# The head of a three-layer kernel on one core: which transfers are issued first and by which queue, the probabilities loaded once, and transposes of the identity placed by the planner

## The chip, the core and the metric

One core of one Trainium2 chip runs the whole program. The metric is device time in microseconds (us) of one execution; the table below gives the median of three timed runs. Engines are named as in the profile: PE (TensorE matmul), PEld (its weight loads), DVE (VectorE), ACT (ScalarE), POOL (GpSimd), SP (SyncE). A "q" behind a name (SPq) is the engine's instruction queue, from which transfers are issued.

## The reference, cut

```python
def _attn_ref(q, k, v, p):            # q, k, v: (4, 8, 576, 64), p: (4, 8, 32, 64)
    p_packed = sm_attn(p, k, v)       # softmax(p k^T / 8) v : 32 packed rows for each head
    return sm_attn(q, p_packed, p_packed)

def _moe_ref(x, domain_probs, w1, w2):        # x: (2304, 512), 4 experts, F = 1024
    p = domain_probs / (domain_probs.sum(-1, keepdims=True) + 1e-09)
    for e in range(E):
        out += p[:, e:e + 1] * (np.maximum(x @ w1[e], 0.0) @ w2[e])

def _moe2_ref(x, phi, w1, w2):                # 8 experts of 4 slots each
    logits = x @ phi                          # softmax over rows (dispatch), over slots (combine)
    slot_out[e] = np.maximum((d.T @ x)[e] @ w1[e], 0.0) @ w2[e]
    return c @ slot_out

def reference(**kwargs):                      # attention, then _moe_ref, then _moe2_ref
    return _moe2_ref(_moe_ref(_attn_ref(...)))
```

## The kernel before

The program is written out by hand in the order in which each engine shall work. The second attention is never formed in full: with packed rows `pkn` (32 for each head) and weights `a2` (softmax of q against them), the first layer's x @ w1 is a2 @ (pkn @ w1). `make_g(ci)` computes g = pkn @ w1 for one half expert (512 columns of w1, one transfer of 1 MB into a tile `w1` of which there is one buffer), splits it into two fp32r parts, and then issues the next w1 transfer. `mm1(s)` computes h = relu(a2 @ g) for 128 columns, times the probability of the expert (`pe_t`), which is `ht`; there are 32 such slots for each of the 4 batch entries. `logits(ci)` needs w2 @ phi in place of w2: `wphi_ops(n, ...)` makes it for one of 8 chunks of w2 (1 MB each, n = 0 to 7): four groups of four transposes on PE (`turn`, psum tile `w2t{n}_x`), each copied out by ACT (`put`), a projection by phi of 32 small matmuls (`project`, psum tile `pw`), one transpose back (`wp`), copied out twice by ACT. The chunks lie in 4 buffers `w2s`; chunk n + 4 is loaded when chunk n has been projected.

The head, which the change touches, is everything up to the first `mm1`: the attention of batch entry 0 for two groups g of four heads, `make_g(0)`, the normalised probabilities, and as many of the `wphi_ops` as fit. The attention of one group runs: k transposed in 32x32 blocks by DVE (`kf`), scores p k^T on PE (`sa`), maximum, exponential, normalisation (`mx`, `ex`, `norm`), transposes on PE (`turn`, psum `et`), p_packed on PE (`pv`), packed into `pkn`, q transposed by DVE (`qf`), scores q pkn^T on PE (`sb`), and a softmax over 32 rows by DVE, ACT and POOL (`nat`, `sub`, `xp`, `add`, `mul`, `fl`), whose result is split into `a2` (`hi` on ACT, `lo` on DVE). `place_ops` orders these steps: every step has an engine, an expected cost and its predecessors; the planner takes the step that could begin first and issues its instructions, so the order on each engine is fixed when the program is built, by the planner's numbers. Steps of rank 2 (the `wphi_ops`) fill in; what of them is not placed when the rest is done is left in `rest` and issued two at a time between the `mm1` slots (`wphi_rest`).

All transfers of the head are issued by SP in the order of the `load(...)` calls, but for the probabilities, which POOL issues: `load_probs` reads the same 36 KB four times, once for each 32 partitions. SP issues in order: a transfer that must wait holds all behind it. Behind the planned part SP issues p, k and v of batch entry 1 (`load_p(1)`, `load_two`, `load_v(1, 0)`), then the third w1 half (`w1_2`). Tiles in `hr` are the ring that later takes h; in the head its parts hold q, v, w2 and the attention's intermediate tiles, so many rows name `hr`.

## Time and profile before

| | us |
|---|---|
| median of 3 timed runs | 516.65 (515.19 to 517.91) |
| the profiled execution | 512.97 |
| its span (first to last instruction) | 511.2 |
| PE busy in the span | 467.6 (91%) |
| PE matmuls of the h products (L620) | 221.6 |
| DMA read | 98.78 MB |

The sums below are made against the profiled execution (512.97 us). The span is 1.8 us shorter than that execution; the median of the timed runs is 3.7 us longer. Times inside the trace count from the first instruction. A row of the time line gives start, duration, engine, line, operation, what it writes and reads, and in brackets how long its engine had waited and what ended the wait. A row of the chain of waits gives start, duration and what the end of the program was waiting for in that stretch.

### The profile page before, as it was taken

How to read it: one execution, taken by the hardware profiler on the slowest of the kernel's cores; microseconds unless marked ns; L12 is line 12 of the kernel's file. 1: busy time of each engine (PE TensorE's matmuls, PEld its weight loads, DVE VectorE, ACT ScalarE, POOL GpSimd, SP SyncE). 2: the span in 40 equal slices, each digit the busy share in tenths (PEclk: the TensorE clock that was granted, in tenths of full speed). 3: DMA queues.
4: the chain of work that ended last, by engine and by line, in shares of the span. 5: the costliest groups of instructions: out<-in, count | busy, mean ns of one | idle time of the engine just before them, and what ended most of it. 6: DMA issues, size and time to landing. Idle time of an engine off the chain costs nothing.

```text
span 511.2 us, 13177 instructions
## 1 busy us (share of the span) xinstructions
PE 467.6 (91%) x5572; PEld 332.1 (65%) x5572; DVE 295.0 (58%) x551; ACT 185.4 (36%) x446; POOL 204.4 (40%) x266
## 2 busy tenths in 40 slices
PE   6899899999999989999998999999999985999683
PEld 3778767778775767787665877865878755322142
DVE  4674346688762977778278788754866533140022
ACT  2476445434432433455133445432443200320023
POOL 3024333458743635595244449642765505000000
PEclk8799999999999999999998999999999996899986
DMA  8999634555430555732234522591934499699997
GB/s 200 388 315 288 255 131 140 139 133 166 139 112 3 164 159 147 184 132 86 82 130 130 131 83 83 179 345 58 357 136 165 163 346 418 267 403 394 385 382 251
DMA packets 61836, 104.36 MB, mean 204 GB/s; under 512 B 5904, under 2 KB 24848, under 8 KB 61776
## 3 DMA queue, kind: packets, MB, share of 16 engines
q1 hardware_dynamic: 61648, 103.36, 59.9%
q8 instruction: 44, 0.72, 0.6%
q0 software_dynamic: 128, 0.15, 0.2%
q14 instruction: 16, 0.13, 0.1%
HBM read 98.78 MB, written 4.72 MB: 202 GB/s over the span
## 4 chain that ended last, share of the span: by engine, by line
PE 69%; DMA 17%; DVE 6%; SPq 3%; ACT 2%; issue 1%; POOL 1%; ACTq 0%; POOLq 0%; DVEq 0%
PE h L620 36%; DMA w<-in_moe_w_dram 8%; PE pb L775 8%; PE lg L653 6%; PE g L585 6%; DMA hr<-in_moe_w_dram 4%; DMA ck<-in_moe_w_dram 3%; SPq L849 2%; PE w2t L260 2%; PE sa L358 2%; PE so L1246 1%; DMA hr<-in_v_dram 1%; PE tt L1133 1%; PE o L1284 1%; PE pw L275 1%; PE pv L455 1%
## 5 line engine op out<-in xcount | busy, mean ns | idle before, releaser
L631 POOL TENSOR_TENSOR ht<-ht,pe 128x288 f32<-128x288 f32 x192 | 153.0, 806 | 180.3 <-ACT ht L630 180.2
L620 PEld LDWEIGHTS h<-a,g 128*128 128x128 f32 x1536 | 206.6, 188 | 23.0 <-issue 14.6
L620 PE MATMUL h<-a,g 128*128 128x288 f32 x1536 | 221.6, 299 | 0.0
L630 ACT ACTIVATE ht<-h 128x288 f32<-128x288 f32 x192 | 79.0, 412 | 173.8 <-PE h L620 166.2
L641 DVE STREAM_TRANSPOSE hr<-ht 128x576 f32<-128x576 f32 x128 | 97.3, 763 | 45.2 <-POOL ht L631 41.8
L597 DVE TENSOR_TENSOR g<-g,g 128x512 fp32r<-128x512 f32 x64 | 40.9, 679 | 26.0 <-ACT g L595 26.0
L625 DVE SCALAR_TENSOR_TENSOR ht<-h,pe 128x288 f32<-128x288 f32 x64 | 28.0, 438 | 37.8 <-PE h L620 37.8
L595 ACT CAST g<-g 128x512 fp32r<-128x512 f32 x64 | 34.5, 589 | 28.5 <-PE g L585 28.5
L775 PE MATMUL pb<-hr,d 32*32 32x512 f32 x1152 | 40.6, 598 | 0.0
L585 PE MATMUL g<-w,pkn 64*32 64x512 f32 x512 | 35.8, 600 | 4.2 <-DMA w<-in_moe_w_dram 4.1
L653 PE MATMUL lg<-ht,wphi 128*32 128x288 f32 x512 | 38.3, 412 | 0.0
L653 PEld LDWEIGHTS lg<-ht,wphi 128*32 128x32 f32 x512 | 13.5, 109 | 33.2 <-POOL ht L631 22.5
L775 PEld LDWEIGHTS pb<-hr,d 32*32 32x32 f32 x1152 | 18.9, 103 | 14.3 <-issue 9.2
L1246 PE MATMUL so<-hr,hm 128*32 128x256 f32 (+1 forms) x136 | 18.5, 458 | 4.6 <-DMA hr<-in_moe_w_dram 4.6
L1267 DVE TENSOR_TENSOR rr<-sr,rr 32x256 fp32r<-32x256 f32 x4 | 1.7, 424 | 34.5 <-ACT rr L1265 34.5
L267 ACT COPY hr<-w2t 128x512 f32<-128x512 f32 x32 | 17.5, 598 | 5.3 <-PE w2t L260 5.2
L260 PE MATMUL w2t<-ident,hr 128*128 128x128 f32 x128 | 18.1, 288 | 0.2 <-ACT hr L267 0.2
L260 PEld LDWEIGHTS w2t<-ident,hr 128*128 128x128 f32 x128 | 15.4, 149 | 2.9 <-issue 0.9
L673 POOL COPY ps<-dpn 128x576 f32<-128x576 f32 x16 | 10.7, 667 | 13.5 <-DVE dpn L195 13.5
L789 DVE SCALAR_TENSOR_TENSOR tacc<-tacc,rsc,pb 128x512 f32<-128x512 f32 x12 | 8.2, 744 | 13.2 <-PE pb L775 13.2
L1246 PEld LDWEIGHTS so<-hr,hm 128*32 128x32 f32 x136 | 6.1, 116 | 13.5 <-DMA hr<-in_moe_w_dram 9.3
L1133 PE MATMUL tt<-fold,tacc 128*128 128x64 f32 x32 | 7.1, 423 | 7.7 <-POOL fold L1114 7.7
(161 smaller groups left out, 444.8 us busy)
## 6 DMA issues: line engine op xcount, KB each, us to landing
w<-in_moe_w_dram SPq DMA_DIRECT2D x32, 1024.0 KB, 5.1
hr<-in_moe_w_dram SPq DMA_DIRECT2D x40, 512.0 KB, 8.8
ck<-in_moe_w_dram SPq DMA_DIRECT2D x38, 512.0 KB, 7.6
hr<-in_moe_w_dram SPq DMA_DIRECT2D x8, 1024.0 KB, 9.9
k<-in_k_dram SPq DMA_DIRECT2D x16, 288.0 KB, 4.4
v<-in_v_dram SPq DMA_DIRECT2D x18, 192.0 KB, 6.3
q<-in_q_dram SPq DMA_DIRECT2D x12, 288.0 KB, 2.9
out_dram<-ob SPq DMA_DIRECT2D x8, 384.0 KB, 5.6
```

The source lines that it names most:

```text
L260: pe.transpose(st[x][:, 128 * dc : 128 * dc + 128], t[:, x, 128 * dc : 128 * dc + 128], ident,)
L585: pe.matmul(ps[g][c : c + 32, :], pkn_t[b][o : o + 64, g, hp, 0, :], t[o : o + 64, 2 * g + hp, :], start=True, stop=True, tile_position=(o ...
L595: act.copy(gg[:, 0, g], ps[g])
L597: dve.tensor_tensor(out=gg[:, 1, g], in0=ps[g], in1=gg[:, 0, g].bitcast(F32), op=ALU.subtract)
L620: pe.matmul(ps[:, :HS], gg[:, l, g, fs], m[:, ts], start=(g == 0 and i == 0), stop=(g == 1 and i == 2),)
L625: dve.scalar_tensor_tensor(out=ht[:, ts], in0=ps[:, :HS], scalar=0.0, in1=pr[:, ts], op0=ALU.max, op1=ALU.mult,)
L630: act.activation(out=ht[:, ts], in_=ps[:, :HS], func=AF.Relu)
L631: pool.tensor_tensor(out=ht[:, ts], in0=ht[:, ts], in1=pr[:, ts], op=ALU.mult)
L641: dve.transpose(out=hr[:, place(b, i), :, f0 : f0 + 32], in_=ht_t[s].rearrange("p (x t) -> p x t", t=32),)
L653: pe.matmul(lg_t[b][r][32 * x : 32 * x + 32, :HS], wphi[:, NFT * e + 4 * hf + x, :], ht_t[4 * ci + x][:, HS * r : HS * r + HS], start=(ch ...
L775: pe.matmul(pb[c][m : m + 32, :], d[o, x + par, :], hr[o, lo : hi + 1 : hi - lo, x + par, :], start=(x == 0), stop=(x == NBLK - 2), tile_p ...
L1246: pe.matmul(so[32 * e : 32 * e + 32, d0 : d0 + dw], hm[s][:, x + xl, e, :], cks[e][:, dw * xl : dw * xl + dw], start=(s == 0 and x + xl == 0),
```

## The change

Seven edits, all ahead of the first `mm1`:

1. p of batch entry 0 is issued by ACT as its first instructions, and no longer by SP.
2. SP begins with k. Then come phi and the first w2 chunk, then v and q of group 0 with the probabilities between them, v and q of group 1, w2 chunks 1 and 2, w1_0, w2 chunk 3. The planner counts 2.6 us for 1 MB and adds to each a time until it has landed (`late`).
3. k is transposed in two steps (`kf0`, `kf1`), each as soon as its half is there.
4. The probabilities are loaded once, into 32 partitions, by SP; they are normalised there in three DVE steps, and POOL copies them to the other 96 partitions (`copy_probs`).
5. During the head seven psum banks serve the planner instead of six.
6. The 16 identity transposes at the start (`warm`) go; instead, whenever the planner sees PE wait, it fills the wait with as many (`idle`), into bank 7. There are 17 at the start and 32 more in ten places.
7. Behind the head nothing else is written differently; the `wphi_ops` left over begin at another point.

```diff
-                sp.dma_start(
+                (sp if b else act).dma_start(
...
     def load_probs():
-        for c in range(4):
-            pool.dma_start(
-                dpn[32 * c : 32 * c + 32].rearrange("p b (r x) e -> p (b r) (x e)", r=2),
-                dprobs.rearrange("(b r t x) e -> t (b r) (x e)", b=NB, r=2, x=XR),
-            )
+        sp.dma_start(
+            dpn[0:32].rearrange("p b (r x) e -> p (b r) (x e)", r=2),
+            dprobs.rearrange("(b r t x) e -> t (b r) (x e)", b=NB, r=2, x=XR),
+        )
...
+    def copy_probs():
+        for c in range(1, 4):
+            pool.tensor_copy(dpn[32 * c : 32 * c + 32], dpn[0:32])
...
+            if o.eng == "PE":
+                idle(free.get("PE", 0.0), t)
+            free[o.eng] = t + o.cost
+            o.end = t + o.cost + o.late
...
+        @op(0, "DVE", 0.7, *landed("k0"))
+        def kf0():
+            flip("k", 0)
+
+        @op(0, "DVE", 0.7, kf0, *landed("k1"))
+        def kf1():
+            flip("k", 1)
             late("k")
...
+        load_p(0)
+        load(("p", 0), 0.0, lambda: None, late=3.6)
         for g in range(2):
...
+            for hp in range(2):
+                load((f"k{hp}", g), 0.3, lambda g=g, hp=hp: load_qk(k, "k", 0, g, hp), late=2.2)
...
-        wp = mm_ps("warm")
-        for _ in range(16):
-            pe.transpose(wp[:, :128], ident, ident)
+        def idle(t0, t1):
+            n = int((t1 - max(t0, 1.4)) / (0.213 if t1 < 6 else 0.109))
+            wp = bank(7, "warm") if n > 0 else None
+            for _ in range(n):
+                pe.transpose(wp[:, :128], ident, ident)
```

SP's queue from the last of the four k transfers on, before (`in_moe_w2_dram` is w2, `in_moe_w1_dram` is w1, `tacc` takes phi):

```order
L138 DMA k011_159<-in_k_dram 128x576
L147 DMA hr_109<-in_v_dram 32x8x192 x6
L138 DMA hr_109<-in_q_dram 128x576 x2
L244 DMA hr_109<-in_moe_w2_dram 128x4x512
L138 DMA hr_109<-in_q_dram 128x576 x2
L913 DMA tacc_107<-in_moe2_phi_dram 128x4x32
L244 DMA hr_109<-in_moe_w2_dram 128x4x512
L176 DMA w1_0_339<-in_moe_w1_dram 128x4x512
L244 DMA hr_109<-in_moe_w2_dram 128x4x512 x3
L176 DMA w1_1_490<-in_moe_w1_dram 128x4x512
L244 DMA hr_109<-in_moe_w2_dram 128x4x512
```

The same stretch now:

```order
L140 DMA k011_135<-in_k_dram 128x576
L924 DMA tacc_107<-in_moe2_phi_dram 128x4x32
L256 DMA hr_109<-in_moe_w2_dram 128x4x512
L149 DMA hr_109<-in_v_dram 32x8x192 x3
L184 DMA dpn_105<-in_moe_domain_probs_dram 32x8x36
L140 DMA hr_109<-in_q_dram 128x576 x2
L149 DMA hr_109<-in_v_dram 32x8x192 x3
L140 DMA hr_109<-in_q_dram 128x576 x2
L256 DMA hr_109<-in_moe_w2_dram 128x4x512 x2
L178 DMA w1_0_441<-in_moe_w1_dram 128x4x512
L256 DMA hr_109<-in_moe_w2_dram 128x4x512 x3
L178 DMA w1_1_585<-in_moe_w1_dram 128x4x512
```

p no longer stands in front of k; one w2 chunk stands ahead of v; w1_0 stands behind w2 chunks 1 and 2 instead of behind chunk 1; and w1_1 stands behind w2 chunk 5 instead of ahead of it.

PE in the attention of entry 0, from the transposes of the probabilities to the first `sb`, before (the last digit of `et`, `pv` and `sb` names is a half or group; `w2t0_x` are chunk 0's transposes):

```order
L419 MATMUL et000_229<-ident_103,hr_109 96x128 x4
L419 MATMUL et001_230<-ident_103,hr_109 96x128 x2
L455 MATMUL pv00_242<-hr_109 64x32 x24
L419 MATMUL et010_275<-ident_103,hr_109 96x128 x4
L419 MATMUL et011_276<-ident_103,hr_109 96x128 x2
L260 MATMUL w2t0_0_291<-ident_103,hr_109 128x128 x4
L260 MATMUL w2t0_1_297<-ident_103,hr_109 128x128 x4
L260 MATMUL w2t0_2_303<-ident_103,hr_109 128x128 x4
L455 MATMUL pv01_311<-hr_109 64x32 x24
L358 MATMUL sb000_342<-hr_109,pkn0_156 32x288
```

The same stretch now, from the last transposes of chunk 0 on:

```order
L272 MATMUL w2t0_3_246<-ident_103,hr_109 128x128 x4
L954 MATMUL warm_251<-ident_103 128x128 x4
L434 MATMUL et000_256<-ident_103,hr_109 96x128 x4
L434 MATMUL et001_257<-ident_103,hr_109 96x128 x2
L954 MATMUL warm_275<-ident_103 128x128 x5
L434 MATMUL et010_281<-ident_103,hr_109 96x128 x4
L434 MATMUL et011_282<-ident_103,hr_109 96x128 x2
L954 MATMUL warm_293<-ident_103 128x128
L470 MATMUL pv00_295<-hr_109 64x32 x24
L954 MATMUL warm_334<-ident_103 128x128 x9
L470 MATMUL pv01_344<-hr_109 64x32 x24
L370 MATMUL sb000_376<-hr_109,pkn0_142 32x288
```

Chunk 0's transposes moved from between the two `pv` to ahead of `et`, and identity transposes stand where they were and ahead of each step.

PE around the first h products, before (`h0_0` is slot 0, first half; `wp1` and `pw2` belong to w2 chunks 1 and 2):

```order
L260 MATMUL w2t2_3_513<-ident_103,hr_109 128x128 x4
L260 MATMUL w2t3_0_521<-ident_103,hr_109 128x128 x4
L291 MATMUL wp1_528<-ident_103,pt1_519 128x128
L260 MATMUL w2t3_1_530<-ident_103,hr_109 128x128 x4
L260 MATMUL w2t3_2_536<-ident_103,hr_109 128x128 x4
L275 MATMUL pw2_544<-hr_109,tacc_107 32x128 x16
L620 MATMUL h0_0_585<-a2_00_509,g0_388 128x288 x3
L620 MATMUL h0_0_585<-a2_01_541,g0_388 128x288 x3
L620 MATMUL h0_1_594<-a2_00_509,g0_388 128x288 x3
L620 MATMUL h0_1_594<-a2_01_541,g0_388 128x288 x3
L585 MATMUL g1_0_604<-w1_1_490,pkn0_156 32x512 x2
```

And now:

```order
L287 MATMUL pw1_528<-hr_109,tacc_107 32x128 x16
L954 MATMUL warm_550<-ident_103 128x128 x2
L272 MATMUL w2t3_0_553<-ident_103,hr_109 128x128 x4
L272 MATMUL w2t3_1_559<-ident_103,hr_109 128x128 x4
L303 MATMUL wp1_566<-ident_103,pt1_548 128x128
L272 MATMUL w2t3_2_571<-ident_103,hr_109 128x128 x4
L954 MATMUL warm_577<-ident_103 128x128
L272 MATMUL w2t3_3_579<-ident_103,hr_109 128x128 x4
L954 MATMUL warm_587<-ident_103 128x128 x3
L287 MATMUL pw2_591<-hr_109,tacc_107 32x128 x16
L272 MATMUL w2t4_0_611<-ident_103,hr_109 128x128 x4
L635 MATMUL h0_0_640<-a2_00_521,g0_505 128x288 x3
```

The fourth group of chunk 3 and the first of chunk 4 moved ahead of h0. Behind h0 follows in both programs the second g (`g1`, which needs w1_1), and now `pw3` stands between `g1` and slot 1. In the stretch up to the third g (`g2`) the new order has chunk 4's projection (`pw4`, `wp4`) too, which stands behind `g2` before.

## Rows read from the trace of the kernel before

**Rows 1.** Chain of waits, in order of time: start us, us, what.

```profile
14.43 11.93 DMA w<-in_moe_w_dram
...
44.70 7.88 DMA w<-in_moe_w_dram
52.72 1.09 PE g L585 x16
...
54.92 0.92 PE pw L275 x32
...
60.62 0.87 PE w2t L260 x8
61.49 1.59 PE h L620 x12
```

**Rows 2.** Busy time in stretches of the head and behind it; columns in the first line.

```profile
core 0: us, PE busy (x) PEld busy (x) DVE busy (x) ACT busy (x) POOL busy (x), PEclk, DMA share, GB/s
4.80:7.10 2.30, 0.01 (x1) 0.00 (x0) 0.78 (x1) 0.00 (x0) 0.76 (x3) 1.00 1.06 350
9.30:12.00 2.70, 2.55 (x40) 0.61 (x24) 1.90 (x5) 0.58 (x3) 0.00 (x0) 0.64 1.12 236
18.00:21.70 3.70, 3.70 (x20) 3.58 (x18) 2.44 (x5) 2.51 (x7) 0.67 (x1) 0.53 1.08 388
21.70:25.40 3.70, 3.66 (x114) 2.75 (x112) 2.55 (x8) 1.34 (x5) 0.00 (x0) 1.00 1.05 408
29.90:32.60 2.70, 2.49 (x25) 1.83 (x18) 2.60 (x5) 2.70 (x8) 0.00 (x0) 1.00 0.53 75
52.70:66.40 13.70, 12.80 (x166) 10.66 (x166) 5.22 (x8) 6.35 (x15) 3.41 (x5) 1.00 0.50 192
```

**Rows 3.** Time line of SP's queue, first 46 us.

```profile
0.74 1.81 SPq L159 DMA_DIRECT2D p<-in_p_dram  x4
2.60 1.87 SPq L138 DMA_DIRECT2D k<-in_k_dram  x4
...
16.33 14.21 SPq L244 DMA_DIRECT2D hr<-in_moe_w_dram  x3
30.64 0.45 SPq L176 DMA_DIRECT2D w<-in_moe_w_dram  x1
34.38 0.37 SPq L244 DMA_DIRECT2D hr<-in_moe_w_dram  x1
```

**Rows 4.** What SP's queue waited for, 0 to 53 us: us, times, longest.

```profile
SPq L244 <- PE pw L275: 12.5, 2, 9.3
```

**Rows 5.** DMA issues, KB, us to landing: to 53 us; at 30.6; at 34.4.

```profile
hr<-in_moe_w_dram SPq DMA_DIRECT2D x8, 1024.0 KB, 9.9
...
dpn<-in_moe_domain_probs_dram POOLq DMA_DIRECT2D x4, 36.0 KB, 3.3
...
w<-in_moe_w_dram SPq DMA_DIRECT2D x1, 1024.0 KB, 8.3
...
hr<-in_moe_w_dram SPq DMA_DIRECT2D x1, 1024.0 KB, 7.7
```

**Rows 6.** Time line of DVE and PE, single rows between 1 and 57 us.

```profile
1.36 3.45 PE L933 MATMUL warm<-ident 128*128 128x128 f32 x16 [1.36 <-POOL ident masks.py:199]
...
7.23 1.70 DVE L344 STREAM_TRANSPOSE hr<-k 128x576 f32<-128x576 f32 x2 [0.15 <-DMA k<-in_k_dram]
...
9.33 0.78 DVE L344 STREAM_TRANSPOSE hr<-k 128x576 f32<-128x576 f32 x1 [0.41 <-DMA k<-in_k_dram]
...
21.04 0.78 DVE L344 STREAM_TRANSPOSE hr<-hr 128x576 f32<-128x576 f32 x1 [1.19 <-DMA hr<-in_q_dram]
...
23.31 2.05 PE L358 MATMUL sb<-hr,pkn 32*32 32x288 f32 x64
...
36.81 0.76 DVE L542 TENSOR_TENSOR a<-hr,a 128x576 fp32r<-128x576 f32 x1 [0.80 <-ACT a L537]
...
37.38 1.86 PE L620 MATMUL h<-a,g 128*128 128x288 f32 x12
...
39.17 1.09 PE L585 MATMUL g<-w,pkn 64*32 64x512 f32 x16
...
52.72 1.09 PE L585 MATMUL g<-w,pkn 64*32 64x512 f32 x16 [1.56 <-DMA w<-in_moe_w_dram]
...
56.23 0.33 PE L291 MATMUL wp<-ident,pt 128*128 128x128 f32 x1 [0.44 <-ACT pt L286]
```

More of the change, by code (lines that the diff above doesn't have):

```diff
@@ L87, in mm_ps @@
     def mm_ps(name, keep=False):
-        i = min((i for i in range(6) if i not in kept), key=lambda i: idle_since[i])
+        i = min((i for i in range(nbank[0]) if i not in kept), key=lambda i: idle_since[i])
         clock[0] += 1
@@ L204, in __init__, with place_ops @@
             self.end = None
-    def place_ops(ops, lag=0.2):
-        free, banks_at, left = {}, [0.0] * 6, list(ops)
+    def place_ops(ops, idle, lag=0.2):
+        free, banks_at, left = {}, [0.0] * nbank[0], list(ops)
         while any(o.rank < 2 for o in left):
@@ L225, in place_ops @@
             t, _, n, o = first
-            o.end = free[o.eng] = t + o.cost
+            if o.eng == "PE":
+                idle(free.get("PE", 0.0), t)
+            free[o.eng] = t + o.cost
+            o.end = t + o.cost + o.late
             banks_at = sorted(banks_at)[o.take :] + [o.end] * o.give
@@ L366, in scores @@
             st["ps"] = ps
-        @op(0, "DVE", 1.5, *landed("k"))
-        def kf():
-            for hp in range(2):
-                flip("k", hp)
+        @op(0, "DVE", 0.7, *landed("k0"))
[4 more added lines that the diff above has]
+            flip("k", 1)
             late("k")
-        @op(2, "PE", 1.2, kf, take=2)
+        @op(2, "PE", 1.2, kf1, take=2)
         def sa():
@@ L891, in tile_packed_attention_moe_softmoe, with load @@
         ops = []
-        def load(key, mb, fn, rank=0, deps=()):
-            o = Op(0, "SP", 2.5 * mb, fn, deps, rank=rank)
+        def load(key, mb, fn, rank=0, deps=(), late=2.2):
+            o = Op(0, "SP", 2.6 * mb, fn, deps, rank=rank, late=late)
             ops.append(o)
@@ L961, in tile_packed_attention_moe_softmoe @@
         spread = spread_p(0)
-        ops.append(Op(0, "DVE", 1.7, norm_probs, [loads["k", 1]], rank=1))
+        probs = norm_probs()
+        ops.append(Op(0, "DVE", 0.48, lambda: next(probs), [loads["dp"]], rank=1))
+        ops.append(Op(0, "DVE", 0.87, lambda: next(probs), ops[-1:], rank=1))
+        ops.append(Op(0, "DVE", 0.38, lambda: next(probs, None), ops[-1:], rank=1))
+        ops.append(Op(0, "POOL", 1.2, copy_probs, ops[-1:], rank=1))
         ops.append(Op(0, "POOL", 0.7, lambda: next(spread), ops[-1:], rank=1))
@@ L976, in tile_packed_attention_moe_softmoe @@
                 after = Op(
-                    0, "SP", 2.5, lambda m=m: load_w2(m, w2s[m % W2_BUFS]), [], rank=2
+                    0, "SP", 2.6, lambda m=m: load_w2(m, w2s[m % W2_BUFS]), [], rank=2, late=2.2
                 )
@@ L981, in tile_packed_attention_moe_softmoe @@
             ops.append(Op(0, "NONE", 0.0, done, ops[-1:], rank=2))
-        rest = place_ops(ops)
+        rest = place_ops(ops, idle)
         for o in list(rest):
@@ L987, in tile_packed_attention_moe_softmoe @@
                 rest.remove(o)
+        nbank[0] = 6
         load_p(1)
```

38 lines of the change are left out of this document (21 added, 17 removed).

## The prediction

> **What bounds the kernel now.** I read the chain of waits first. In the head its long pieces are transfers: w1_0 is waited for from 14.43 on and lands 11.93 us later, at 26.36; w1_2 is issued at 44.70 and lands at 52.58, and the third g starts behind it at 52.72 [rows 1], after PE had stood idle for 1.56 us [rows 6]. Behind that point the chain is PE: from 52.7 to 66.4 PE works 12.80 of 13.70 us while the DMA engines are half idle [rows 2]. So the head is bound by when bytes arrive, the rest by PE, and an edit to the head is worth what it moves g2 (the third g, now at 52.72), plus any PE work that is done before g2 and formerly came behind it.
>
> Then I read the stretches for the state of the DMA engines. They are full early (share 1.06 to 1.12), at 236 GB/s while v moves and about 400 later (408 at 21.7 to 25.4), but from 29.9 to 32.6 they run at 0.53 and 75 GB/s [rows 2]: a hole. The queue of SP shows why. It sits on the row of 16.33 for 14.21 us, and behind it w1_1 is issued only at 30.64 [rows 3]; the wait is for `pw`, 9.3 us in one piece [rows 4], since w2 chunk 4 may be loaded only when chunk 0 has been projected, and chunk 0 came late. Besides, k is issued only at 2.60, behind p [rows 3]. These are two losses of DMA time that the change can touch: the start and the hole.
>
> **The change part by part**, as landing times, since these set the end.
>
> *Start.* k is issued at 0.74 in place of 2.60: 1.86 us earlier [rows 3]. Today the four k land up to 9.33, the last two 2.1 us behind the second (7.2) [rows 6], so 1.05 each; 0.30 MB (288 KB) at 408 GB/s [rows 2] would take 0.72. The four loads of the probabilities by POOL (36 KB each [rows 5]) run beside them and leave this stretch; p (0.13 MB) enters it from ACT's queue. Gain between 0 and 4 x 0.33 = 1.3; I take 1.0, because what leaves is as many bytes as what enters, but in smaller pieces. So the last k lands at 9.33 - 1.86 - 1.0 = 6.4 (bounds 6.1 to 7.5).
>
> The row says that the k transfers were slowed by others beside them. The Trainium skill, page "DMA: Bandwidth & Descriptors", section "Issuing engines are not separate DMA queues", has the rule against this edit: transfers started by different engines interleave on the same 16 DMA engines, and issuing from a second one saves only the issuing time. By that rule the last k would land at 7.4 and everything below 1.0 later; no row here has SP and ACT issuing together.
>
> *The same bytes in another order.* Between the last k (9.33) and the last q of group 1 (21.04) lie v, q, phi and one w2 chunk: 11.7 us [rows 6]. The new order moves the same set in this stretch, plus the single load of the probabilities, for which I put 0.4 (bounds 0.1, 36 KB at 408 GB/s, and 1.0). So the last q lands at 6.4 + 11.7 + 0.4 = 18.5. Then 1.05 MB pieces at 408 GB/s, 2.6 us each: w2_1 21.1, w2_2 23.7, w1_0 26.3, w2_3 28.9, w2_4 31.5, w2_5 34.1, w1_1 36.7. w1_0 is where it was (26.36), since a whole w2 chunk has been put ahead of it; that costs nothing, because w2 has to come anyway.
>
> *The hole.* w2_4 now needs `pw0`, which stands between the two `sb`, about 20 to 21: long before its turn at 28.9. w2_5 needs `pw1`, which stands behind g0: 26.3 + 1.09 + 1.0 = 28.5. Issued then, it has 3.0 us until its turn at 31.5. In the trace w1_1, issued into the hole at 30.64 just behind w2_4, landed 8.3 us later [rows 3, 5]; moving the two takes 5.2, so some 3.1 pass between an issue and its first bytes. That is even: I expect no hole worth counting, with nothing to spare. SP now holds w1_1 behind this wait.
>
> *The chain of the attention.* `sb` begins at 23.31, h0 at 37.38, a2 of group 1 is complete at 37.57 [rows 6]; from the last q (21.0) to that a2 are 16.5 us. PE is at the low clock in 18.0 to 21.7 (0.53, so near 1.2 GHz) and at 2.4 GHz from 21.7 on [rows 2]. After the last q at 18.5 the same chain ends at 35.0 at worst; the w2 transposes that stand between the `pv` today are ahead of them now, and `sb` starts some 2 us nearer to q, so about 33. h0 then starts near 33 instead of 37.38. That is ahead of w1_1, so this chain is hidden. The new wait is g1, directly behind h0: h0 ends near 35 and PE waits for w1_1 until 36.7. Of the 4 us that h0 gains, g1 (39.17 now [rows 6]) keeps 2.5.
>
> *From g1 to g2.* In the new order: g1 1.0, `wp2` 0.1, `pw3` 1.0, four h slots of 1.59, `wp3` 0.1, three groups of transposes at 0.87/2, `pw4` 1.0 and `wp4` with its wait 0.6 [rows 1, 6]: 1.0 + 0.1 + 1.0 + 6.4 + 0.1 + 1.3 + 1.0 + 0.6 = 11.5. So g2 at 36.7 + 11.5 = 48.2. It needs w1_2. Today that lands 10.5 us after w2_5 (34.38 + 7.7 = 42.1 [rows 5]; 52.58 [rows 1]), with p, k and v of entry 1 between; now the same set follows w1_1: 47.2. Hidden by 1.0.
>
> *Work moved ahead of g2.* `pw4` and `wp4` stand behind g2 now: 0.92, a wait of 0.44 and the transpose [rows 1, 6], 1.5 in all.
>
> *Cost at nothing.* Normalising 32 partitions takes DVE the same columns; POOL's three copies and the spread have until h0, some 15 us. The table load on ACT comes 1.8 us later, and ACT's first exponential needs the scores of k, which lands at 6.4 at the earliest for the last. The 33 more identity transposes: 3.45/16 = 0.22 us each at the start, 0.11 (0.87/8) at the full clock [rows 6, 1], 3.6 to 7.1 in all; they stand in waits for transfers, and up to g1 there are 1.7 us of slack. If that cover were missing, they would be the cost. The low clock of 9.3 to 21.7 (0.64, 0.53 [rows 2]) is paid in the shade of transfers already, so its going is worth only what the attention chain has above.
>
> **Sum.** 52.72 - 48.2 = 4.5, plus 1.5: 6.0; I take off 0.3 for the fillers and ACT's fuller queue around g1. The gain is 5.7: 512.97 becomes 507.3, and the median 516.65 becomes **511.0** (the median lies 3.7 above the profiled execution; I move both by the same amount).
>
> **The rivals.**
>
> *A, only the issue time is won at k*, or the probabilities cost 1.0 in the new place. Everything lands 1.0 later: gain 4.7, **512.0**. For it: p enters the stretch of k, in pieces as small as ever. Against: what leaves is of the same size.
>
> *B, the hole comes back* at w2_5, since SP must now wait for `pw1` before it can issue w1_1. For it: exactly this wait cost 9.3 us of SP's time [rows 4], and there is no margin. Against: `pw1` needs only w1_0 and copies of ACT that are early. A hole of 2.5, as now, gives 3.2: **513.4**.
>
> *C, the clock.* PE falls to the low clock after waits such as 4.8 to 7.1 (busy 0.01) and is there from 18.0 to 21.7 although it is busy [rows 2]. If identity transposes do not hold it up and PE works at 1.2 GHz from w1_0 on, then g0, `pw1`, four groups, `pw2`, one group and h0, 1.1 + 1.0 + 1.7 + 1.0 + 0.4 + 1.6 = 6.8, take 13.6; g1 starts at 39.9, 3.2 late: gain 2.5, **514.1**. Against: at 21.7 the clock was up again after work of the same kind.
>
> *D, slower: w1_0 is late.* Three 1 MB loads stand ahead of it instead of two, and w1_0 frees g0, that `pw1`, that w2_5, and that w1_1 behind it. From w1_0 at 27 on, each us costs one; from 33 the change is no gain. If all moved as slowly as v (236 GB/s [rows 2]), the 0.04 + 3.15 MB behind q would take 13.5 instead of 8.2, w1_0 would land at 32 and w1_1, with 5.2 for that chain (1.1 + 1.0 + 3.1) and two chunks of 4.4, at 46: g2 at 57.5, gain -3.3, **519.9**. Against: behind v the rate is 388 to 408 in two stretches [rows 2].
>
> **Chances.** The forecast 0.57 (its own range 509.5 to 512.5), A 0.16, B 0.13, C 0.08, D 0.03, and 0.03 for what I don't see. For 8 in 10 the range reaches from 508.3 (the last k at 6.1, a cheap load of the probabilities, no loss at g1, and the 1.4 us by which the timed runs differ) to 514.2 (B and C, partly). A measurement of this kernel tells some 0.5% (2.6 us) from no change: below 514.1 I put 0.82, above 519.2 0.04, and 0.14 between.
>
> **What would show it.** Right: k's last transposition near 6.5; no stretch of low DMA share before 45 us; the wait of SP for `pw` down from 9.3 to below 3; h0 near 33; PE waiting 1 to 3 us at g1 for w1_1, near 36.7; g2 near 48 without a wait. Behind g2 the two traces should run alike, 6 us apart. Wrong: w1_0 after 27.5, a hole between w2_4 and w2_5, a granted clock below 1 between 22 and 36, or time that is won at g2 and lost again later, for which I see no place in the trace.

## The result, and the profile after

The change makes the kernel slower by about half a per cent: 518.9 us in the median of 20 runs (511.9 to 523.9) against 514.5 for the kernel before (20 runs), with a ratio of 1.0055 and an interval of 1.0029 to 1.0082. Six of the 20 runs, of 520.3 us and more, the first profiled one among them (523.61), count as slow and are left out of the ratio; the median of the other 14 is 517.6. A later set of runs gave the same ratio, 518.0 against 514.5, 1.0055 (1.0019 to 1.0090). The forecast was 511.0, and faster.

The rows below are of a second profile of the changed kernel (518.08 us, span 516.3), whose head goes the same way as the first one's. The forecast times of the head beside what the two profiles show, in us from the first instruction:

| | before | forecast | after, 1st | after, 2nd |
|---|---|---|---|---|
| last k lands | 9.30 | 6.4 | 6.83 | 6.88 |
| last q lands | 21.01 | 18.5 | 22.76 | 21.72 |
| w1_0 lands | 26.36 | 26.3 | 30.82 | 29.87 |
| w2 chunk 5 issued | 34.38 | 28.5 | 35.80 | 34.78 |
| w1_1 lands | 38.98 | 36.7 | 45.38 | 44.18 |
| h0 begins | 37.38 | 33 | 40.06 | 39.01 |
| g1 begins | 39.17 | 36.7 | 45.51 | 44.32 |
| g2 begins | 52.72 | 48.2 | 59.08 | 57.79 |

I read the chain of waits first, as before [rows 1]. Chain of the changed kernel (start, duration, what):

```profile
2.15 4.91 DMA p<-in_p_dram
...
21.94 1.54 issue
23.49 0.71 PE pv L470 x7
...
35.24 8.94 DMA w<-in_moe_w_dram
44.18 0.14 issue
44.32 1.96 PE g L600 x16
...
57.86 1.02 PE g L600 x16
```

The long piece is w1_1, issued at 35.24 and 8.94 us under way; g1 hangs on it. w1_2, the long piece of before (7.88 us), no longer stands in the chain.

What SP's queue waited for up to 53 us, and its time line (start, duration; a row runs to the last issue of its group):

```profile
SPq L256 <- PE pw L287: 13.7, 3, 6.5
```

```profile
18.40 1.06 SPq L178 DMA_DIRECT2D w<-in_moe_w_dram  x1
19.51 15.64 SPq L256 DMA_DIRECT2D hr<-in_moe_w_dram  x3
35.24 0.46 SPq L178 DMA_DIRECT2D w<-in_moe_w_dram  x1
```

The wait for `pw` is there as before (12.5 us, 9.3 the longest [rows 4]), and as before w1_1 stands behind it. But w1_1 now stands behind chunk 5, which waits for `pw1`, where before it stood behind chunk 4, which waited for `pw0`. The row of 15.64 us ends with chunk 5's issue. The two issues between 34.5 and 35.7, with KB and the time to landing:

```profile
hr<-in_moe_w_dram SPq DMA_DIRECT2D x1, 1024.0 KB, 5.5
w<-in_moe_w_dram SPq DMA_DIRECT2D x1, 1024.0 KB, 8.9
```

Stretches of the head (columns in the first line); they answer to [rows 2]:

```profile
core 0: us, PE busy (x) PEld busy (x) DVE busy (x) ACT busy (x) POOL busy (x), PEclk, DMA share, GB/s
9.00:12.00 3.00, 3.00 (x49) 1.05 (x39) 1.64 (x4) 0.30 (x1) 0.00 (x0) 1.00 1.11 282
12.00:16.00 4.00, 4.00 (x47) 3.08 (x28) 2.42 (x9) 2.53 (x10) 0.00 (x0) 1.00 1.00 256
16.00:20.00 4.00, 4.00 (x72) 3.79 (x71) 2.91 (x6) 2.88 (x8) 0.00 (x0) 1.00 0.90 264
...
34.50:37.00 2.50, 2.50 (x27) 2.04 (x20) 2.12 (x5) 2.50 (x7) 1.37 (x1) 1.00 0.46 26
```

Two things are to be seen. From 9 to 20 us the DMA engines are full or nearly so (share 0.90 to 1.11) and move 256 to 282 GB/s, where before reached 388 from 18 us on. And the hole is back, now at 34.5 to 37.0 (share 0.46, 26 GB/s).

PE's time line around it (in brackets: the idle time before, and what ended it):

```profile
7.68 2.80 PE L370 MATMUL sa<-hr,pt 32*32 32x288 f32 x32 [2.43 <-DVE pt L332]
...
20.59 1.35 PE L470 MATMUL pv<-hr 96*64 96x32 f32 x38
23.49 0.71 PE L470 MATMUL pv<-hr 96*64 96x32 f32 x10 [1.54 <-issue]
...
28.87 3.66 PE L272 MATMUL w2t<-ident,hr 128*128 128x128 f32 x32
...
32.57 1.09 PE L600 MATMUL g<-w,pkn 64*32 64x512 f32 x16
33.59 1.08 PE L287 MATMUL pw<-hr,tacc 128*32 128x128 f32 x32
...
44.32 1.96 PE L600 MATMUL g<-w,pkn 64*32 64x512 f32 x16 [3.46 <-DMA w<-in_moe_w_dram]
...
57.79 1.09 PE L600 MATMUL g<-w,pkn 64*32 64x512 f32 x16
```

w1_0 had landed at 29.87, but g0 begins at 32.57: PE was late, and 32 transposes stand ahead of g0 on it. `pw1` follows g0 and ends at 34.67, SP issues chunk 5 at 34.78, and w1_1 behind it.

Behind the head these two traces take the same time: from g2 to the last g 337.4 us before (52.7 to 390.1) and 337.3 now (57.8 to 395.1), and from there to the end 121.1 and 121.2. In this profile the loss of 5.1 us is in the head. A single profile's time behind the head is not sharp, though: from g2 to the end the profiles of this case took 455.5 to 462.7 us, the first profile of the changed kernel 462.7. So g2 says what a head is worth, and the medians whether it reaches the end.

### The profile page after: what moved, and what is told of

The parts are those of the page before. It is cut to its first block, busy times and chain, and to the rows that moved or that the text cites. A ratio compares the mean times of both kernels' runs of the same rounds, so it can differ in the third digit from the quotient of the medians.

```text
span 521.8 us, 13239 instructions
## 1 busy us (share of the span) xinstructions
PE 473.7 (91%) x5605; PEld 335.3 (64%) x5605; DVE 296.2 (57%) x551; ACT 185.2 (35%) x446; POOL 202.8 (39%) x265
## 4 chain that ended last, share of the span: by engine, by line
PE 68%; DMA 18%; DVE 7%; SPq 2%; issue 1%; ACT 1%; POOL 0%; ACTq 0%; POOLq 0%; DVEq 0%
PE h L635 36%; PE pb L790 7%; PE lg L668 6%; DMA w<-in_moe_w_dram 6%; PE g L600 6%; DMA ck<-in_moe_w_dram 5%; DMA hr<-in_moe_w_dram 4%; DMA hr<-in_v_dram 3%; SPq L864 2%; PE sa L370 2%; PE pv L470 2%; PE pw L287 1%; PE sb L370 1%; PE tt L1160 1%; PE w2t L272 1%
## 5 line engine op out<-in xcount | busy, mean ns | idle before, releaser
L635 PEld LDWEIGHTS h<-a,g 128*128 128x128 f32 x1536 | 208.0, 189 | 24.1 <-issue 15.1
L610 ACT CAST g<-g 128x512 fp32r<-128x512 f32 x64 | 34.5, 590 | 30.4 <-PE g L600 30.4
L1273 PE MATMUL so<-hr,hm 128*32 128x256 f32 (+1 forms) x136 | 17.0, 421 | 4.8 <-DMA hr<-in_moe_w_dram 4.8
L272 PE MATMUL w2t<-ident,hr 128*128 128x128 f32 x128 | 16.7, 275 | 0.2 <-DMA hr<-in_moe_w_dram 0.2
L272 PEld LDWEIGHTS w2t<-ident,hr 128*128 128x128 f32 x128 | 14.2, 140 | 1.9 <-issue 0.7
L600 PEld LDWEIGHTS g<-w,pkn 64*32 64x32 f32 x512 | 6.5, 104 | 13.8 <-issue 10.4
L1273 PE MATMUL so<-ck,hm 128*32 128x512 f32 (+1 forms) x52 | 12.9, 533 | 1.7 <-DMA ck<-in_moe_w_dram 1.7
```

Source lines behind the costliest of these rows:

```text
L272: pe.transpose(st[x][:, 128 * dc : 128 * dc + 128], t[:, x, 128 * dc : 128 * dc + 128], ident,)
L600: pe.matmul(ps[g][c : c + 32, :], pkn_t[b][o : o + 64, g, hp, 0, :], t[o : o + 64, 2 * g + hp, :], start=True, stop=True, tile_position=(o ...
L610: act.copy(gg[:, 0, g], ps[g])
L635: pe.matmul(ps[:, :HS], gg[:, l, g, fs], m[:, ts], start=(g == 0 and i == 0), stop=(g == 1 and i == 2),)
L1273: pe.matmul(so[32 * e : 32 * e + 32, d0 : d0 + dw], hm[s][:, x + xl, e, :], cks[e][:, dw * xl : dw * xl + dw], start=(s == 0 and x + xl == 0),
```

## The experiments

Each run was timed beside the kernel before on the same chip. Times are medians, the ratio is to the kernel before, and the landings are of one profile each.

### The first four: which part of the head loses

The changed kernel once more (its rows stand above):

> The changed kernel as it is, once more, for a profile whose clock can be set beside the kernel before. In its first trace the last q landed at 22.76 (the forecast was 18.5), w1_0 at 30.82, w1_1 at 45.38, g2 began at 59.15, and the first layer norm step behind that was 5.95 us later than before. Theory H (the head's transfers): these times come again within 0.7 us, and the whole is between 1 and 6 us over the kernel before. Theory L (the loss arises late, at windows of low clock that only that run had): the head's times come again or not, but the whole is within 1 us of before.

Theory H holds: the head's times came again within 1.4 us (twice the 0.7 that I allowed), and the whole is 3.4 us over before.

v in one piece (a planner's place and the transfer issued in it are taken apart, so that the engines keep their order):

```diff
-            load(("v", g), 0.9, lambda g=g: load_v(0, g, flat[1][:, 1536 * g : 1536 * g + 1536]))
+            load(("v", g), 0.9, lambda: next(turns)())     # q and the probabilities likewise
+        turns = iter([v_of(0), v_of(1), load_probs, q_of(0), q_of(1)])
```

> One thing changed: behind the first w2 chunk SP issues the six transfers of v together, then the probabilities, then both q; the order on the computing engines is that of the changed kernel. Theory M (the transfers of v, in 768-byte packets, slow whatever shares the DMA engines with them, and standing in two pieces between q and w2 they do it twice): last q near 19.5 (18.5 to 20.5) in place of 22.8, everything behind it 2 to 4 us earlier, g2 near 56. Theory P (the one load of the probabilities in 144-byte packets is what slows this stretch): last q stays at 22 to 23, g2 at 58.5 to 59.5.

Measured: last q 19.72, w1_0 27.54, g2 55.48; 514.8 us, 1.0013 (0.9984 to 1.0042). As theory M said in this one profile; but the repetitions below show the same order at 22.31, and the time is told apart neither from the kernel before nor clearly from the changed kernel.

The probabilities behind q:

```diff
+        turns = iter([v_of(0), q_of(0), v_of(1), q_of(1), load_probs])
```

> One thing changed: the load of the probabilities stands behind both q instead of between v and q of group 0; their normalisation moves back with it. Theory P (that load in 144-byte packets slows the stretch): last q near 19 to 20 in place of 22.8 and w1_0 near 27 to 28. Theory M (v's own packets, in two pieces, do it): last q at 22 to 22.8, w1_0 within 0.7 us of 30.8.

Measured: last q 22.34; w1_0 32.05, 1.2 us beyond the first profile's; 516.0 us, 1.0025 (0.9997 to 1.0053). Nothing of the 3 us that theory P expected came, so the 144-byte packets are not borne out as what slows the stretch.

w1_1 ahead of chunk 5:

```diff
         w1_t[n] = t
+        while n and held:
+            held.pop()()
...
+        def w2_after(m):
+            if m == 5:
+                held.append(lambda: load_w2(m, w2s[m % W2_BUFS]))
+            else:
+                load_w2(m, w2s[m % W2_BUFS])
```

> One thing changed: the load of w2 chunk 5 is issued behind that of w1_1 instead of ahead of it, so that w1_1 no longer stands behind the wait for pw1; all else is the changed kernel. Theory Q (SP's wait and the place behind it are what makes w1_1 late): w1_1 is issued as soon as g0 is done, near 34.7, and lands near 41 (40 to 42) in place of 45.4; g1 begins 3 to 4 us earlier, g2 near 56, the whole 2 to 3.5 us faster than the changed kernel. Theory C (the chain of the attention would hold g1 anyway): g1 comes no more than 1 us earlier and the whole stays.

Measured: 511.8 us, 0.9950 (0.9917 to 0.9984), 6.2 us less than the changed kernel, more than theory Q said. SP's time line and the issue at 30.66:

```profile
30.66 0.37 SPq L178 DMA_DIRECT2D w<-in_moe_w_dram  x1
31.66 0.37 SPq L260 DMA_DIRECT2D hr<-in_moe_w_dram  x1
```

```profile
w<-in_moe_w_dram SPq DMA_DIRECT2D x1, 1024.0 KB, 5.4
```

w1_1 is issued at 30.66 in place of 35.24, takes 5.4 us in place of 8.9, and lands at 36.04; g1 then follows h0 (36.13) without a wait, and g2 begins at 50.34. Not all of this is the swap. PE's second `pv` began as late as in the changed kernel (20.80 against 20.59), but the stop of 1.54 us did not come, the granted clock was 1.00 from 21 to 29 us, and g0 began 3.1 us earlier than there:

```profile
20.80 1.59 PE L474 MATMUL pv<-hr 96*64 96x32 f32 x48
...
29.45 1.09 PE L604 MATMUL g<-w,pkn 64*32 64x512 f32 x16
```

Counted from g0, w1_1 is issued 1.2 us behind it instead of 2.7, and lands 6.6 us behind it instead of 11.6: the swap is worth these 5.0 us of landing. This profile is also of the fastest of the twelve runs (507.8). In 34.5 to 37.0 the DMA engines now move 401 GB/s:

```profile
34.50:37.00 2.50, 2.50 (x45) 2.13 (x44) 1.87 (x3) 2.20 (x6) 0.00 (x0) 1.00 1.04 401
```

### Both edits, and what the other parts of the change are worth

> The two edits of the earlier runs together: v in one piece behind the first w2 chunk, and the load of w1_1 ahead of that of w2 chunk 5; all else is the changed kernel. Theory S (the two losses are separate and add up): last q near 19.7, w1_0 near 27.5, w1_1 issued near 30 and landed near 35.5, h0 near 35.2 with g1 right behind it (near 37), g2 at 49 to 50 and then held by PE's own work; some 0.7 to 1 us faster than the version with w1_1 first alone (511.8), so near 511. Theory O (w1_1 alone decides, the stream of v is then hidden): g2 and the time as with w1_1 first alone, 50.3 and 511.8 within 0.5.

Measured: last q 22.31, w1_0 30.05, w1_1 38.95, g2 51.53; 511.7 us, 0.9943 (0.9913 to 0.9972). In the time theory O (g2 fits neither): v in one piece adds nothing to the swap that can be measured. But here the last q came at 22.31 with the same order of transfers that had given 19.72.

Without the 32 identity transposes (`for _ in range(n if t1 < 6 else 0)`):

> The changed kernel without the 32 identity transposes behind the first 17 (they compute nothing that is used). Theory F0 (they stand in waits and do nothing for or against): the time stays within 1 us of the changed kernel (518), the gap of 1.5 us inside the second pv stays. Theory F1 (they take PE's time on the path): g0, pw1 and w1_1 come 0.5 to 1.5 us earlier and so does g2. Theory F2 (they hold the clock up): windows of low clock between 12 and 45 us that the changed kernel doesn't have, and g2 later by 1 us or more.

Measured: last q 22.79, g2 57.84; 515.9 us, 1.0019 (0.9983 to 1.0054), not told apart from the changed kernel. The 1.54 us gap in `pv` did not come. The granted clock was low, as F2 said, here at 0.56 and 0.58, but g2 did not move:

```profile
21.00:25.00 4.00, 3.20 (x58) 2.90 (x66) 1.47 (x2) 0.36 (x2) 1.71 (x4) 0.56 1.05 405
25.00:29.00 4.00, 4.00 (x88) 2.20 (x80) 2.61 (x6) 0.52 (x3) 0.00 (x0) 0.58 1.05 405
```

With the transposes it was low as well, in the second profile of the changed kernel 0.82 and 0.75 (in the first 1.00 and 0.57):

```profile
21.00:25.00 4.00, 2.46 (x58) 1.85 (x62) 1.64 (x4) 0.62 (x3) 1.93 (x4) 0.82 1.01 339
25.00:29.00 4.00, 4.00 (x91) 2.09 (x76) 2.87 (x7) 0.27 (x1) 0.00 (x0) 0.75 1.05 403
```

p issued by SP again, on the version with both edits:

```diff
-                (sp if b else act).dma_start(
+                sp.dma_start(
```

> The version with both edits, but p of entry 0 issued by SP ahead of k again, as in the kernel before; the order on the computing engines stays. Theory I (issuing k 1.9 us earlier is what the start gained): last k 1.5 to 2.5 us later (near 8.5 to 9), last q 1.5 to 2 us later. Theory B (the DMA engines are loaded by bytes from 2.5 us on, and who issues matters little): last k at most 1 us later and last q within 0.8 us; the transposed p is there some 2.5 us earlier, since p lands near 4.1 instead of 7.0.

Measured: last k 8.75 (2.0 later than with both edits, as theory I said), last q 22.39 (level with the 22.31 of the profile above, as B said, but 2.5 later than in the repetition below, so the landings don't decide); 510.7 us, 0.9930 (0.9902 to 0.9958). In the time p on ACT's queue brings nothing that can be measured.

w1_0 ahead of chunk 2:

```diff
-            if n == W2_BUFS - 1:
+            if n == W2_BUFS - 2:
                 load("w1", 1.0, load_w1)
```

> The version with both edits, and w1_0 loaded ahead of w2 chunk 2 instead of behind it; the planner orders the computing engines anew. Theory W (what bounds the head is how early w1_0 frees g0 and its buffer): w1_0 lands near 25, g0 near 25.5, w1_1 issued near 27 and landed near 33, so before h0; g2 held by the attention chain and PE alone, 47 to 49. Theory A (h0 and the work ahead of g2 bound it already): g2 within 0.7 us of the version with both edits.

Measured: w1_0 25.81, w1_1 issued at 27.27 but landed only at 36.28, since three w2 chunks stood ahead of it; g2 50.09, which is neither W's 47 to 49 nor within A's 0.7 us of 51.53; 512.6 us, 0.9958 (0.9928 to 0.9988). In the time no gain over both edits.

### What makes the stream slow

> The kernel before, once more, for a second profile of its head. If the time that the transfers of the head take is set by their order, v lands near 14.4, the last q near 21.0 and g2 begins near 52.7 again, each within 0.5 us. If it varies from one execution to the next by itself, as 19.7 and 22.3 for the last q in two profiles with the same order of transfers suggest, the last q lies up to 2 us off in either direction, and g2 with it. Ratio 1.00.

Measured: v 14.41 as before, last q 19.60, w1_0 26.42 against 26.36, g2 53.42 against 52.72; ratio 0.9978 (0.9944 to 1.0012). The q that was last came 1.4 us earlier, but phi (21.39 for 21.18) and w1_0 behind it did not: the sum of the bytes arrives at the same time. So the landing of a single transfer varies by more than the 0.5 us that I allowed for one order, and g2 came 0.7 us later.

v in long rows, 32 partitions each:

```diff
-                t[32 * l : 32 * l + 32, :].rearrange("p (h x) -> p h x", x=192),
+                t[32 * l : 32 * l + 32, :],
+                v[b, 4 * g : 4 * g + 4].rearrange("h (a s) d -> (h a) (s d)", s=24)[32 * l : 32 * l + 32],
```

> The changed kernel with v of entry 0 loaded in another form: each of the three transfers of a group still writes 32 partitions, but in rows of 6144 contiguous bytes in place of eight rows of 768; the rows of v so go to wrong places, and the attention of entry 0 is computed from them. All transfers stay in their places. Theory R (the short packets are what slows the stretch in which v moves): the stretch from 10 to 20 us runs near 400 GB/s and the last q lands near 17.5 in place of 21 to 22.8. Theory T (writing into 32 partitions slows it, whatever the packets): last q at 20.5 or later, as now.

v over 96 partitions in one transfer:

```diff
-        for l in range(3):
+                t[:96, :].rearrange("p (h x) -> p h x", x=192),
+                v[b, 4 * g : 4 * g + 4].rearrange("h (r p x) d -> p (h r) (x d)", r=2, x=3),
```

> The changed kernel with v of entry 0 loaded in yet another form: one transfer for each group, over 96 partitions, still in rows of 768 bytes; the rows of v go to other places than they should within each group of three, and the attention of entry 0 is computed from them. Theory T (32 partitions slow it): the stretch of v runs near 350 GB/s and the last q lands near 18. Theory R (the short packets): last q at 20.5 or later, with packets of 768 bytes at 45 ns and more.

Measured: with long rows last q 19.52, 303 and 290 GB/s in 9 to 12 and 12 to 16 us: neither 17.5 nor 20.5. With 96 partitions last q 18.99, w1_0 26.67, the earliest of all with this order. The packets' own records say more: 6144-byte packets took 234 ns when the first of them ran and some 460 ns once many of them ran side by side; with all 16 engines on v that is 16 x 6144 B / 460 ns = 214 GB/s. The 768-byte packets took 56 ns on average in the kernel before, 16 x 768 / 56 = 219 GB/s. Eight times the size takes eight times as long, so theory R falls: what fits these packet times is that writing 32 partitions at a time sets v's rate, though the last q, at 19.52, did come earlier with the long rows. Over 96 partitions the 768-byte packets took 44 ns (279 GB/s), beside other transfers. The whole did not measurably gain by it: 516.7 us, 1.0040 (1.0005 to 1.0074), and 517.0 us, 1.0030 (0.9987 to 1.0073). w1_1 still stood behind chunk 5, it landed at 40.22 and 39.37, and g1 waited 3.33 and 2.73 us for it. The profile with 96 partitions is of the fastest of its ten runs (508.9 to 519.3), so its landings need not be those of the median run.

v directly behind k and phi, on both edits:

```diff
-        turns = iter([v_of(0), v_of(1), load_probs, q_of(0), q_of(1)])
+        turns = iter([v_of(0), v_of(1), lambda: load_w2(0, w2s[0]), load_probs, q_of(0), q_of(1)])
-        load("w2", 1.0, lambda: load_w2(0, w2s[0]))
+        load("w2", 1.0, lambda: next(turns)())
```

> The version with both edits, and one thing more: the six transfers of v are issued ahead of the first w2 chunk, right behind k and phi, as they stand behind k in the kernel before; the computing engines keep their order but for a few rows. Theory X (what makes the stream slow and uneven is that v, which writes 32 partitions at a time, runs beside transfers over 128 partitions that are still under way): w2 in packets of 2048 bytes takes near 84 ns each, not 97 to 112, and the last q lands at 19 to 19.6. Theory Y (the stream is uneven by itself): anywhere between 19.7 and 22.8, w2 packets at 97 ns or more.

Measured: last q 18.26, w1_0 27.00. Stretches of this kernel:

```profile
7.00:9.00 2.00, 1.00 (x24) 0.41 (x28) 1.50 (x3) 0.00 (x0) 0.00 (x0) 1.00 1.09 233
9.00:12.00 3.00, 3.00 (x57) 1.02 (x41) 1.96 (x5) 0.66 (x3) 0.00 (x0) 0.57 1.11 239
12.00:16.00 4.00, 2.02 (x26) 1.21 (x11) 2.76 (x10) 1.49 (x6) 0.00 (x0) 0.90 1.06 383
16.00:20.00 4.00, 4.00 (x24) 3.94 (x23) 2.39 (x5) 1.21 (x3) 0.00 (x0) 0.57 1.05 408
```

This fits theory X in kind (the last q came even earlier than it said, w2's packets took longer): v by itself runs at 233 to 239 GB/s for some 5 us, and then everything else at 383 to 408. In the changed kernel the slow rate lasts from 9 to 20 us, and packets of q and w2 take longer beside v (by the packets' records, q's of 2304 bytes took 98 ns on average here, 165 and 122 in the two profiles of the changed kernel; chunk 0's of 2048 bytes 94 here, not the 84 that I expected, and 107 in both there). But the kernel is not faster than with both edits alone, 512.8 us, 0.9965 (0.9936 to 0.9994): PE's order puts chunk 0's transposes ahead of the attention, and they now wait for chunk 0:

```profile
15.41 2.94 PE L276 MATMUL w2t<-ident,hr 128*128 128x128 f32 x16 [1.98 <-DMA hr<-in_moe_w_dram]
...
21.37 1.59 PE L474 MATMUL pv<-hr 96*64 96x32 f32 x48
```

The first `pv` stands at 16.82 where both edits are made without this one (the repetition below), and h0 at 34.81 instead of 39.35.

> The version with both edits once more. Theory Y or a skew that differs from one execution to the next: last q somewhere between 19.7 (one profile with this order of transfers) and 22.3 (another). If the order alone sets it: 22.3 again, w1_0 at 30. Time near 511.7.

Measured: last q 19.85, w1_0 27.57, w1_1 35.45, h0 34.81, g1 36.58, g2 48.95; 511.2 us, 0.9924 (0.9892 to 0.9955). So one order of transfers gives 19.7, 22.3 and 19.9. The changed kernel's own order gave 20.6 to 22.8 in four profiles; the two ranges overlap, so it is not shown that v in two pieces is worse than v in one. Its stretches, and below them those of the earlier profile of the same kernel:

```profile
12.00:16.00 4.00, 4.00 (x45) 4.00 (x38) 2.79 (x10) 3.40 (x12) 0.00 (x0) 1.00 1.12 268
16.00:20.00 4.00, 4.00 (x84) 3.62 (x82) 3.22 (x8) 2.80 (x8) 0.00 (x0) 1.00 1.04 401
```

```profile
12.00:16.00 4.00, 3.11 (x33) 2.72 (x26) 2.73 (x9) 2.14 (x6) 0.00 (x0) 0.97 1.06 214
16.00:20.00 4.00, 4.00 (x72) 3.79 (x71) 0.28 (x1) 2.41 (x6) 0.00 (x0) 1.00 1.04 231
```

Where v overlaps chunk 0 for longer (chunk 0 landed at 10.98 and at 13.81), both are slower. What decides how long they overlap in one execution stays open.

This repetition also gives the cleanest view of the swap. Beside the version with v in one piece alone it differs by the swap only, and the two streams came alike: w1_0 at 27.57 and 27.54, g0 at 28.13 and 28.48, no stop of PE. Without the swap w1_1 landed at 40.61 instead of 35.45, and g2 began at 55.48 instead of 48.95. The g1 and the stretch from 40 to 46 us, without the swap:

```profile
40.75 1.96 PE L600 MATMUL g<-w,pkn 64*32 64x512 f32 x16 [3.75 <-DMA w<-in_moe_w_dram]
...
40.00:46.00 6.00, 5.25 (x53) 2.91 (x54) 1.97 (x3) 1.51 (x4) 0.00 (x0) 0.50 0.92 240
```

And with it, with its g2:

```profile
36.58 1.09 PE L604 MATMUL g<-w,pkn 64*32 64x512 f32 x16
48.95 1.09 PE L604 MATMUL g<-w,pkn 64*32 64x512 f32 x16 [0.24 <-DMA w<-in_moe_w_dram]
...
40.00:46.00 6.00, 6.00 (x71) 5.84 (x73) 2.97 (x6) 3.55 (x8) 3.81 (x5) 1.00 1.03 241
```

Of the 6.5 us at g2, 4.2 are g1's later start and 2.4 the stretch behind it, in which PE worked at a granted clock of 0.50 after the wait of 3.75 us. In the time the swap is worth 3.1 to 3.6 us here (514.8 against 511.7 and 511.2; the intervals of the ratios do not overlap).

### The swap on the kernel before, and orders built on the finding

The same swap with chunk 4 (`if m == 4`):

> The kernel before with one thing changed: the load of w2 chunk 4 is issued behind that of w1_1 instead of ahead of it, as the version of the changed kernel did with chunk 5. Theory G (the change's other edits are worth next to nothing, and what the better versions gain is this swap): w1_1 is issued near 27.7 and lands near 33, the hole goes, w1_2 lands near 50 and g2 begins near 50.5, and the time is 2 us or more under the kernel before, near 512, like the changed kernel with the same swap (511.8). Theory K (before does not hang on w1_1, since g1 follows h0 without a wait, and the new order is worth something by itself): within 1 us of the kernel before, 2 us or more above the changed kernel with the swap.

Measured: w1_1 landed at 34.38, but g1 begins at 39.51 behind h0 as ever, w1_2 lands at 53.00, g2 begins at 53.13; 514.4 us, 0.9980 (0.9948 to 1.0012). Theory K: the kernel before did not hang on w1_1. So, by the medians, the rest of the change is worth something once the swap is made; whether that is the order of the transfers, the order of the work on the engines or another part was not taken apart, and the interval overlaps those of the swapped versions of the changed kernel.

v and q ahead of chunk 0, with the planner's order following, and the same with p on SP:

```diff
+        for g in range(2):
+            load(("v", g), 0.9, v_of(g))
+        for g in range(2):
+            load(("q", g), 0.6, q_of(g))
         load("w2", 1.0, lambda: load_w2(0, w2s[0]))
```

> The version with w1_1 first, and the head's transfers in the order k, v, q, w2 chunk 0, phi, probabilities, then as before; the planner orders the computing engines anew. Theory X: last q near 16, w1_0 near 27, sb near 18 to 19, h0 near 35, g2 49 to 50.5 and held by PE's own work, time at or below the version with both edits (511.7). Theory Y: last q at 17 to 20, w1_0 28.5 or later, time 512 to 514.

> As the version with v and q first, but p of entry 0 issued by SP ahead of k. Theory B (the start is a matter of bytes, not of who issues): last q and w1_0 0.5 to 1.2 us later than with p on ScalarE's queue, time within 0.7 us of it. Theory I (k's issue counts in full): all landings 1.9 us later, time 1 us or more above it.

Measured: last q 15.38 and 18.49, w1_0 27.07 and 29.49, g2 53.36 and 51.65; 514.6 us, 1.0000 (0.9967 to 1.0033), and 512.9 us, 0.9974 (0.9942 to 1.0005). The stream of the first went near to what X said, the time did not: h0 began at 37.50 and 36.29, behind a wait of 1.48 us for ACT in both. With p on SP the last q and w1_0 landed 3.1 and 2.4 us later, more than either theory said, and the kernel was no slower, against theory I.

The two better versions without the identity transposes:

> The version with both edits without the 32 identity transposes behind the first 17 (they compute nothing that is used). Theory F0 (they are worth nothing in a head that waits for transfers): landings as with them (last q near 19.8 or up to 22.3), g2 within 0.7 us of 48.9 to 51.5, time within 1 us of 511.4. Theory F2 (they hold the clock up for the attention chain, which counts once w1_1 is in time): windows of low clock between 20 and 35 us, g0 or h0 1 us or more later against their transfers than with them, time 1.5 us or more above.

> The version with both edits and p issued by SP ahead of k, without the 32 identity transposes: what is left of the change is the order of the transfers, the single load of the probabilities, k in two steps and the seventh psum bank. If the transposes and p on ScalarE's queue bring nothing: 510 to 512.5, as with them (510.7 and 511.7). If both help a little: 513 or more.

Measured: 511.8 us, 0.9952 (0.9923 to 0.9981), and 510.6 us, 0.9919 (0.9882 to 0.9955). Neither the transposes nor p on ScalarE's queue bring anything that these runs can measure. The versions with both edits beat both kernels; their ratios of 0.992 to 0.995 are not told apart from one another.

## Why the prediction was wrong

**The start: within its bounds, empty in its effect.** The last k landed at 6.83 and 6.88, for 6.4 with bounds of 6.1 to 7.5. The rule of the Trainium skill, page "DMA: Bandwidth & Descriptors", section "Issuing engines are not separate DMA queues", says that transfers started by different engines interleave, and would have given 7.4. The trace agrees that they interleave, p landing at 4.11 to 7.06 and k at 3.94 to 6.88; the number lies between the two. What I left out is p itself. It landed at 4.07 before, at 7.06 now, and the scores need both. DVE transposes p ahead of three of the k, so these queue behind it (the row of p names phi as what it waited for; p itself had landed at 7.06):

```profile
3.96 0.78 DVE L356 STREAM_TRANSPOSE hr<-k 128x576 f32<-128x576 f32 x1 [3.96 <-DMA k<-in_k_dram]
7.18 0.45 DVE L332 STREAM_TRANSPOSE pt<-p 128x256 f32<-128x256 f32 x1 [2.45 <-DMA tacc<-in_moe_phi_dram]
7.55 2.05 DVE L356 STREAM_TRANSPOSE hr<-k 128x576 f32<-128x576 f32 x3
```

PE's first scores begin at 7.68; before, at 7.12 or 7.13.

**"The same bytes in another order": the first step that failed.** 11.7 + 0.4 us became 14.8 (6.88 to 21.72) and 15.9. I took the time of a set of transfers as its property. It was one reading to begin with: the kernel before took 11.7, 10.3 and, with its swap, 10.1 us from the last k to the last q. And it depends on what runs side by side: v's slow rate goes with writing 32 partitions at a time, packets of q and chunk 0 took longer beside it, and the change put chunk 0 ahead of v and q between its pieces. With v by itself behind k the step comes out: 7.11 to 18.26 is 11.2 us. That two pieces are worse than one is not shown.

**The hole: the second step that failed.** I had chunk 5 issued at 28.5, w1_0 + g0 + `pw1`, and no hole. It was issued at 34.78: w1_0 was 3.6 us late (29.87 for 26.3), and from its landing to the end of `pw1` 4.8 us passed, not 2.2, since g0 stood behind PE's attention chain and 32 transposes (PE was busy without a break from 23.49 to 32.57, after the gap of 1.54, at the low clock up to some 29 us). From there w1_1 took 9.5 us to land instead of 8.2. 3.6 + 2.6 + 1.3 = 7.5, and 44.18 - 36.7 = 7.5. "That is even, with nothing to spare" was the point to stop at: a time that waits on four others has no forecast without a margin. The swap shows the step by itself: with streams alike, w1_1 landed 5.2 us and g2 began 6.5 us earlier with it. The 2.6 us of PE's lateness belong to executions with the stop or the low clock: in the versions with v in one piece and with w1_1 first, g0 began 0.9 and 1.1 us after w1_0 had landed.

**The rivals.** What happened is B and D together. D had the right chain, w1_0, g0, `pw1`, chunk 5, w1_1: at 32 for w1_0 it gave 46 for w1_1, 57.5 for g2 and 519.9 us; measured were 30.82, 45.38, 59.08 and 518.9, and in the second profile 29.87, 44.18 and 57.79. Its chance of 0.03 was the error. That its numbers came so near is in part luck: it had w1_0 late by a slow stream behind q and nothing of PE being late for g0. I held against it that behind v the rate is 388 to 408, which stayed nearly true (368 from 22 to 26 us, 403 from 25 to 29); the lateness came from ahead of the last q. C's low clock occurred (0.82 and 0.75 in 21 to 29 us), and it was not free. Together with the stop of 1.54 us it is why g0 began 2.7 us after w1_0 had landed: from the second `pv` to g0 passed 12.0 us, and 8.7 where w1_1 was first and the clock stayed at 1.00. Identity transposes did not prevent it, and without them it was lower still and g2 stayed. What share of the loss in the median run is the clock's was not tried.

**The chain of the attention** came later than 33, with the last q, and was hidden as said: h0 at 39.01, g1 at 44.32 after 3.46 us of waiting.

**From g1 to g2** I said 11.5, and w1_2 hidden by 1.0. In the version with both edits it took 12.4 (36.58 to 48.95): PE's own work took 12.1, mis-sized by 0.6 at the full clock, and the last 0.24 were a wait for w1_2, which landed at 48.90 and not at 47.2. In the changed kernel it took 13.5, where the granted clock was 0.84 from 40 to 46. A wait at g1 can so cost more than its length, as the stretch at 0.50 above shows; the prediction had no term for that.

**Work moved ahead: not shown to reach the end.** g2 is 5.07 us later than before in the second profile, but the eighth g only 3.6 (122.0 for 118.4): 1.5 came back. In the version with both edits g2 is 3.8 earlier and the eighth g 5.4 (113.0). But at the last g the two stand at 5.0 later and 3.9 earlier: the 1.5 us is gone again in both. From the eighth g to the last the profiles of this case took 270.1 to 276.3 us, so this can be chance or a loss of its own; the runs don't tell.

**The sum.** g2 at 57.79 instead of 48.2 is 7.5 from w1_1, 2.0 from the stretch behind g1 and 0.1 between the two. With chunk 5 and w1_1 exchanged and v in one piece, the head runs close to what I wrote for the change: w1_1 at 35.45 (36.7), g1 at 36.58 (36.7), g2 at 48.95 (48.2). The whole, 511.2 us for 511.0, meets by luck: the forecast took 5.7 off a median of three runs, 516.65, that was 2.1 above the median of 20, and this version gained 3.4. The forecast was for a kernel with the exchange, and the changed kernel lacked it.

## What to carry to other kernels

Before a transfer is put behind one that must wait, write down what releases that wait and everything that stands ahead of the releaser on its own engine; if the margin is nothing, forecast the hole, or issue the transfer that does not wait first. A rate read from a trace belongs to a transfer and its neighbours: here v, which writes 32 partitions at a time, slowed those that ran beside it; by itself it left them fast, though the time did not gain by that here. An engine's order that fits one sequence of landings (here chunk 0's transposes ahead of the attention) turns into a wait when the landings are improved.
